# One PSUM bank taken from the product with V, given to scores and transpositions, and a plan with slack on banks

## The chip, the core and the metric

The kernel runs on one core of a Trainium2 chip. Its time is the device time of one execution in microseconds (us). TensorE (PE) does matmuls and transpositions and writes them to PSUM, which has eight banks of 512 fp32 columns; VectorE (DVE) and ScalarE (ACT) read PSUM; GpSimd (POOL) works in SBUF alone; SyncE (SP) issues the DMAs. Each engine runs its instructions in the order in which the program holds them, and waits there for what it needs.

## What is computed

Causal attention with a decay bias, over 4 batches, 8 heads, 576 positions and 64 dimensions a head, and then a mixture of 4 experts in which each token takes all of them, weighted by `domain_probs`:

```python
scores = q @ k.transpose(0, 1, 3, 2) / np.sqrt(D)
cum = np.cumsum(np.maximum(s, 0.0), axis=-1)
bias = -(cum[:, :, :, None] - cum[:, :, None, :])
scores = np.where(causal, -1e9, scores + np.minimum(bias, 0.0))
attn = exp(scores - max); attn = attn / (attn.sum(-1) + 1e-9)
x = (attn @ v) as 2304 rows of 8 * 64
p = domain_probs / (domain_probs.sum(-1) + 1e-9)
out = sum over e of p[:, e] * (relu(x @ w1[e]) @ w2[e])      # w1 512x1024, w2 1024x512
```

## The kernel before

**Visits.** Attention goes in 40 visits. The first 8 treat rows 0 to 319 of the heads of batch 0, the next 8 the other rows of these heads, and the last 24 a whole head each. A visit has up to five row blocks. For each block TensorE computes scores into a bank `S` (L584 or L587; blocks of 576 columns in two pieces of 288), VectorE adds the mask and takes the maximum (L597), ScalarE takes the exponential and its sum (L605), GpSimd or VectorE adds 1e-9 to the sum (L611), VectorE inverts it (L613), and GpSimd, ScalarE or VectorE multiplies the block by it (L400 to L402). TensorE then transposes the block's 128x128 pieces into a bank `T` (L632). ScalarE copies the rounded high part `aTh` from it (L407) and VectorE subtracts for the low part `aTl` (L660, L663); with that the bank is free.

**Product with V.** When all of a visit's blocks are transposed, TensorE multiplies by V (L686). `V` holds the high part of V in 64 columns and the low part in the other 64, so the result has two halves, that are added: ScalarE copies one from PSUM into `xr` (L696), VectorE adds the other (L701). A visit of 576 rows doesn't fit one bank of 512 columns, so the tile `pv` has two banks, with its first 256 columns at the end of the first; each V block's product is cut at column 256. Two heads make a pair; its `xr` is split in two parts (`xh`) and stored to `x_d`.

**Between them.** The first expert's two layers (L778 and L791, in banks `mo`), over groups of two or three tiles of tokens, fill TensorE where attention waits. Their inputs `xg` are loaded from `x_d` (L771).

**What sets the order.** The order of all these instructions is not written by hand. A planner (`Sched.run`) plays the tasks through with a duration for each and, on every engine, takes the ready task of the lowest `prio`; what it takes is written at once into the program. A task takes banks from pools and gives them back; a bank given back is free again in the plan 150 ns after the task's end (L286). `sources` says from which pools a bank may come: `S` and `T` have two banks each, and may take a bank `mo` while no filler matmul is ready. The planner stops when attention is done. The rest of the first expert's work is written behind it, with the preparation of the other experts' operands on GpSimd (`sums_of`: for the Strassen-like scheme of those experts GpSimd forms four sums for each of three groups of six tiles, twelve in all, each split in two parts; SP stores each at L916, and loads `xf_d` into `t` at L899 and `x_d` into `x` at L872 for them) placed at fixed counts of matmul time behind the end of attention. Then the other three experts follow, on TensorE without breaks.

Of the kernel before, what the change touches and what calls it, by code (L numbers as in the profile page):

```python
# [57 lines left out]
def t_pe4(n):  # L58
    return max(n / 0.6, 157) + 3
# [6 lines left out]
def t_dve(n):  # L66
    return n / 0.96 + 70
# [20 lines left out]
D6 = 3000  # L88
NWARM = 7
# [65 lines left out]
class Sched:  # L155
# [32 lines left out]
    def sources(self, t, p, lend):  # L188
        if p in ("S", "T") and lend:
            return (p, "mo")  # L190
        if t.prio < 1000.0 * NH + 900:
            return LEND.get(p, (p,))
        return (p,)

    def run(self, until):
# [22 lines left out]
        while left:  # L218
# [3 lines left out]
            for e in names:  # L222
# [62 lines left out]
                for p, k in t.give:  # L285
                    self.pools[self.home.pop((p, k))].append([end + 150, self.tok.pop((p, k))])  # L286
# [18 lines left out]
def body(ctx, tc, qk, vp, s, dp, w1, w1s, w2, w2s, out):  # L305
# [39 lines left out]
    make("pv", 1, [P, 1024], pool=pattn)  # L345
# [152 lines left out]
    prev_v = prev_ad = None  # L498
    for j, (h, ms) in enumerate(VISITS):
# [9 lines left out]
        pv0 = 256 if ext > 512 else 0  # L509
# [158 lines left out]
        mms = []  # L668
        for aT in (aTh, aTl)[0:1 if first else 2]:
            for n in range(nb):  # L670
                if aT is aTl and n == NC - 1:
                    continue
                i0 = max(q0, 128 * n)
# [4 lines left out]
        def f(e, j=j, mms=mms, first=first, pvk=pvk, o=o, pv0=pv0):  # L678
            t = tok[pvk]
            for i, (aT, n, i0, i1) in enumerate(mms):  # L680
                same = [k for k, x in enumerate(mms) if pv0 == 0 or (x[2] >= 256) == (i0 >= 256)]
                if first:
                    st, mv = tok[f"vz{j % 2}", j][:, n, :], tok["aTf", j][:, n, i0:i1]
                else:
                    st, mv = tok["V", j][:, n, :], aT_blocks(aT, tok["par", j], n, n + 1, i0, i1)[:, 0, :]
                nc.tensor.matmul(t[:, pv0 + i0:pv0 + i1], st, mv, start=(i == same[0] and not (first and o)),  # L686
                                 stop=(i == same[-1] and (not first or o > 0)))
        cost = sum(t_pe4(w - u) if first else t_pe(w - u) for _, _, u, w in mms)
        v = sch.add({"PE": cost}, f, evs + [v_ready] + ([prev_v] if first and o else []), prio=base + PO,
                    take=[pvk] if not (first and o) else [], give=[(f"vz{j % 2}", j), ("aTf", j)] if first else [("V", j), ("par", j)])  # L690
        prev_v = v

        r0, r1 = q0, ext
        if not first:
            def f(e, j=j, o=o, r0=r0, r1=r1, pk=pk, pv0=pv0):
                nc.scalar.activation(tok["xr", pk][o:o + 64, r0:r1], tok["pv", j][64 - o:128 - o, pv0 + r0:pv0 + r1], AF.Copy)  # L696
            sh = sch.add({"ACT": t_act(r1 - r0)}, f, [v], prio=base + PO + 10, take=[("xr", pk)] if o == 0 else [])

            def f(e, j=j, o=o, r0=r0, r1=r1, pk=pk, pv0=pv0):
                xr = tok["xr", pk]  # L700
                nc.vector.tensor_tensor(out=xr[o:o + 64, r0:r1], in0=tok["pv", j][o:o + 64, pv0 + r0:pv0 + r1], in1=xr[o:o + 64, r0:r1], op=ALU.add)  # L701
            ad = sch.add({"DVE": t_dve(r1 - r0)}, f, [sh], prio=base + PO + 10, give=[("pv", j)])
        else:
            ad = v
        attn.append(ad)
        if o:
# [3 lines left out]
            def xsrc(pk=pk, r0=r0, r1=r1, first=first, pv0=pv0):  # L710
                return tok["pv", pk][:, pv0 + r0:pv0 + r1] if first else tok["xr", pk][:, r0:r1]
# [570 lines left out]
```

## Time and profile before

| | |
|---|---|
| median of 3 runs | 937.98 us (937.55 to 938.73) |
| the profiled execution | 939.92 us, span 938.1 |
| PE busy in the span | 926.4 us (99%), 6304 matmuls |
| DVE, ACT, POOL busy | 713.6 (76%), 451.6 (48%), 456.8 us (49%) |
| mean granted clock | 0.998 |

A row of the profile names an engine, the line of the kernel, the operation and its tiles (buffer numbers left out), with starts in us from the span's start. `PE` is a matmul, `PEld` the load of its weights, which runs ahead. A matmul's row is longer than the step to the next matmul, since matmuls overlap; their pace is read from the starts. Idle time in brackets is that of the engine just before the instruction, with what ended it. Fp32 matmuls have two rows each in the counts.

### The profile page before, as it was taken

Reading aid. Unit: us, or ns where it says so; the run is one execution under the profiler, and the core shown is the slowest. Engines: PE = TensorE matmul, PEld = TensorE weight load, DVE = VectorE, ACT = ScalarE, POOL = GpSimd, SP = SyncE. Lnnn points to the kernel's source line nnn. Section 1 sums busy time; section 2 is a strip of 40 time slices with the busy share of each in tenths; the row PEclk is TensorE's granted clock in tenths of the full one; section 3 lists DMA queues with packets and bytes.
Section 4 is the critical chain, followed back from the end, with each engine's and each line's share of the span. In section 5 each row is a group of like instructions: output and inputs, shape, how many; then the busy total and the mean of one; then the engine's idle time right before and its main releaser. Section 6 shows DMA issues by size and latency. Waiting matters only on the chain.

```text
span 938.1 us, 17970 instructions
## 1 busy us (share of the span) xinstructions
PE 926.4 (99%) x6304; PEld 882.1 (94%) x6304; DVE 713.6 (76%) x1727; ACT 451.6 (48%) x1036; POOL 456.8 (49%) x503
## 2 busy tenths in 40 slices
PE   9989999999999999999999999999999999999998
PEld 6878898998999988999999999999999999999998
DVE  7978888888886211468779977988797879678976
ACT  6878887787775110252444333434252524443340
POOL 5557575475541689412753173435343714571222
PEclk9999999999999999999999999999999999999999
DMA  5877678677642796596775558654785458744603
GB/s 141 251 209 213 191 184 239 172 207 207 164 125 85 240 388 217 190 318 243 236 240 184 189 185 281 214 177 160 247 279 186 142 197 275 235 154 152 221 30 118
DMA packets 125898, 189.71 MB, mean 202 GB/s; under 512 B 10433, under 2 KB 102113, under 8 KB 125809
## 3 DMA queue, kind: packets, MB, share of 16 engines
q1 hardware_dynamic: 125808, 188.57, 63.3%
q8 instruction: 50, 0.82, 0.4%
q14 instruction: 40, 0.32, 0.1%
HBM read 144.73 MB, written 29.54 MB: 186 GB/s over the span
## 4 chain that ended last, share of the span: by engine, by line
PE 87%; DVE 4%; DMA 3%; issue 2%; ACT 2%; POOL 1%; SPq 0%; DVEq 0%; POOLq 0%; ACTq 0%
PE pb L1079 26%; PE pb L1089 20%; PE mo L1089 8%; PE mo L791 7%; PE mo L778 6%; PE T L632 5%; PE pv L686 5%; PE S L587 4%; PE pb L778 3%; PE pb L791 2%; DMA xg<-x_d 1%; PE S L584 1%; DVE a L597 1%; DVE aTl L660 1%; DMA raw<-in_qk_dram 1%
## 5 line engine op out<-in xcount | busy, mean ns | idle before, releaser
L1079 PE MATMUL pb<-x,w1h 128*128 128x384 f32 x1008 | 256.6, 335 | 0.5 <-ACT t L1119 0.3
L1079 PEld LDWEIGHTS pb<-x,w1h 128*128 128x128 f32 x1008 | 180.8, 188 | 2.5 <-DVE t L1123 1.8
L1079 PE MATMUL pb<-x,w1l 128*128 128x384 f32 x504 | 168.5, 334 | 0.0
L394 POOL TENSOR_TENSOR hT_r<-t,hT_r 128x768 fp32r<-128x768 f32 x18 | 34.0, 1887 | 268.5 <-PE pb L1079 215.5
L1119 ACT ACTIVATE t<-pb 128x384 f32<-128x384 f32 x144 | 66.3, 486 | 160.8 <-PE pb L1079 151.6
L1182 DVE SCALAR_TENSOR_TENSOR acc<-pb,prob,acc 128x256 f32<-128x256 f32 x288 | 126.2, 476 | 5.3 <-PE pb L1089 4.9
L1089 PE MATMUL pb<-w2h,hT_r 128*128 128x256 f32 x720 | 114.6, 283 | 0.1
L402 POOL TENSOR_SCALAR a<-a,sm 128x192 f32<-128x192 f32 (+4 forms) x145 | 83.9, 586 | 57.2 <-DVE sm L613 39.5
L605 ACT ACTIVATE a<-a,mx 64x64 f32<-64x64 f32 (+4 forms) x160 | 89.1, 559 | 23.0 <-DVE mx L597 16.6
L1089 PEld LDWEIGHTS pb<-w2h,hT_r 128*128 128x128 f32 x720 | 99.5, 191 | 0.3 <-issue 0.3
L1123 DVE TENSOR_TENSOR t<-pb,t 128x384 f32<-128x384 f32 x108 | 54.4, 550 | 57.5 <-PE pb L1079 36.1
L1079 PEld LDWEIGHTS pb<-x,w1l 128*128 128x128 f32 x504 | 94.6, 188 | 0.0
L1096 ACT ACTIVATE hT_r<-t 128x768 fp32r<-128x768 f32 x54 | 45.7, 846 | 98.1 <-PE pb L1089 92.6
L1093 DVE SCALAR_TENSOR_TENSOR t<-t 128x768 f32<-128x768 f32 x72 | 88.2, 1226 | 1.7 <-issue 1.6
L778 PE MATMUL mo<-xg,w1h 128*128 128x256 f32 (+1 forms) x368 | 84.9, 309 | 0.0
L407 ACT ACTIVATE aTh<-T 128x256 fp32r<-128x256 f32 (+2 forms) x167 | 65.8, 433 | 22.3 <-PE T L632 17.6
L632 PE MATMUL T<-idn,a 128*128 128x128 f32 x465 | 72.8, 278 | 3.7 <-DVE aTl L660 2.0
L660 DVE TENSOR_TENSOR aTl<-T,aTh 128x256 fp32r<-128x256 f32 (+2 forms) x167 | 72.5, 456 | 5.3 <-ACT aTh L407 4.0
L1089 PE MATMUL pb<-w2l,hT_r 128*128 128x256 f32 x360 | 71.5, 283 | 0.0
L597 DVE CUSTOM_DVE_ANT_0 a<-S,mask 128x320 f32<-128x320 f32 (+4 forms) x151 | 61.6, 420 | 9.7 <-PE S L584 4.4
L632 PEld LDWEIGHTS T<-idn,a 128*128 128x128 f32 x465 | 53.2, 142 | 15.5 <-issue 4.6
L1182 DVE SCALAR_TENSOR_TENSOR acc<-mo,prob,acc 128x256 f32<-128x256 f32 x144 | 62.9, 476 | 1.6 <-PE mo L1089 1.6
(149 smaller groups left out, 2076.3 us busy)
## 6 DMA issues: line engine op xcount, KB each, us to landing
x<-xs_d SPq DMA_DIRECT2D x68, 768.0 KB
x<-x_d SPq DMA_DIRECT2D x55, 768.0 KB
xs_d<-x SPq DMA_DIRECT2D x12, 768.0 KB
raw<-in_qk_dram SPq DMA_DIRECT2D x24, 288.0 KB
KK<-AB_r SPq DMA_DIRECT2D x24, 288.0 KB
x_d<-xh SPq DMA_DIRECT2D x12, 576.0 KB
w1r<-in_w1s_dram SPq DMA_DIRECT2D x6, 1024.0 KB
w2r<-in_w2s_dram SPq DMA_DIRECT2D x6, 1024.0 KB
```

The costliest lines, as they stand in the source:

```text
L402: (nc.gpsimd if e == "POOL" else nc.vector).tensor_scalar(out, in_, scale, 1.0 if bias is None else bias, op0=ALU.mult, op1=ALU.mult if bi ...
L597: nc.vector.tensor_tensor_reduce(out=z[0:n, j0:j1], in0=tok["S", (c, pi)][0:n, 0:j1 - j0], in1=mask[0:n, 448 - a + j0:448 - a + j1], scale ...
L605: nc.scalar.activation(z[0:n, 0:bb], z[0:n, 0:bb], AF.Exp, bias=tok["mx", c][0:n, k:k + 1], scale=-1.0, accum_out=tok["sm", c][0:n])
L632: nc.tensor.transpose(t[:, 128 * k:128 * k + 128], z[:, 128 * x:128 * x + 128], idn)
L660: nc.vector.tensor_tensor(out=dst, in0=src, in1=h_.bitcast(F32), op=ALU.subtract)
L778: nc.tensor.matmul(t[:, 0:w], wl[q][:, dc, o:o + P], xgt[:, l, dc, 0:w], start=(u == 0), stop=(u == 3 * KD - 1))
L791: nc.tensor.matmul(t, ht[:, fc, 128 * ti:128 * ti + 128], wl[fc // 2][:, fc % 2, :], start=(u == 0), stop=(u == 3 * KF - 1))
L1079: nc.tensor.matmul(ts[u][:, 0:TG], wv[wl][:, k, 128 * u:128 * u + 128], x[:, xl_, k, :], start=start and k == 0 and n == 0, stop=k == 1 an ...
L1089: nc.tensor.matmul(ts[t][:, 0:256], h_part(o, hl_)[:, k, 128 * t:128 * t + 128], wv[wl][:, k, :], start=start and k == 0 and n == 0, stop= ...
L1093: (nc.gpsimd if e == "POOL" else nc.vector).scalar_tensor_tensor(out=out, in0=in0, scalar=0.0, in1=in1, op0=ALU.max, op1=op)
L1119: nc.scalar.activation(tmp[name][:, u], ts[u][:, 0:TG], f)
L1182: nc.vector.scalar_tensor_tensor(out=a_, in0=ts[t][:, 0:256], scalar=prob[:, tt, e:e + 1], in1=a_, op0=ALU.mult, op1=ALU.add)
```

## The change

The tile `pv` shrinks to one bank, and the bank set free makes a pool `X` of its own, from which `S` and `T` may take. The product of a visit of 576 rows is done in two tasks: columns 64 to 575 (512 of them, in `pv`) and then columns 0 to 63, which only the first V block reaches, in a bank of `T` (or `X`, or `mo`). Each has its own copy and add. `prev_ad` becomes a list, so that the pair's split waits for both adds. In the plan a bank of `S`, `T`, `X` or `mo` is free 500 ns and not 150 after the task that gives it back, from 45 us of the plan's time on.

```diff
+SPARE = ("S", "T")
+BSLACK = 500
+T_SLACK = 45000
+PSUM_POOLS = ("S", "T", "X", "mo")
...
     def sources(self, t, p, lend):
-        if p in ("S", "T") and lend:
-            return (p, "mo")
+        if p in ("S", "T") and (lend or p in SPARE):
+            return (p,) + ("X",) * (p in SPARE) + ("mo",) * lend
...
-                    self.pools[self.home.pop((p, k))].append([end + 150, self.tok.pop((p, k))])
+                    self.pools[self.home.pop((p, k))].append([end + (BSLACK if p in PSUM_POOLS and now > T_SLACK else 150), self.tok.pop((p, k))])
...
-    make("pv", 1, [P, 1024], pool=pattn)
+    make("pv", 1, [P, 512], pool=pattn)
+    make("X", 1, [P, 512], pool=pattn)
...
-        pv0 = 256 if ext > 512 else 0
+        cut = 64 if ext > 512 else 0
...
-                for u, w in ((i0, min(256, ext)), (max(256, i0), ext)) if pv0 else ((i0, ext),):
-                    if u < w:
-                        mms.append((aT, n, u, w))
...
+        spans = [(max(cut, q0), ext)] + [(0, cut)] * (cut > q0)
+        ads = []
+        v = None
+        for si, (r0, r1) in enumerate(spans):
+            mms = [(aT, n, max(r0, 128 * n), r1) for aT in (aTh, aTl)[0:1 if first else 2] for n in range(nb)
+                   if max(r0, 128 * n) < r1 and not (aT is aTl and n == NC - 1)]
+            bk = ("T", (j, "s")) if si else pvk
...
+                    nc.tensor.matmul(t[:, i0 - c0:i1 - c0], st, mv, start=(i == 0 and not (first and o)),
+                                     stop=(i == len(mms) - 1 and (not first or o > 0)))
...
+            v = sch.add({"PE": cost}, f, evs + [v_ready, v] + ([prev_v] if first and o else []), prio=base + PO,
+                        take=[bk] if not (first and o) else [], give=([(f"vz{j % 2}", j), ("aTf", j)] if first else [("V", j), ("par", j)]) if lastv else [])
...
+                nc.scalar.activation(tok["xr", pk][o:o + 64, r0:r1], tok[bk][64 - o:128 - o, r0 - c0:r1 - c0], AF.Copy)
+            sh = sch.add({"ACT": t_act(r1 - r0)}, f, [v] + ads, prio=base + PO + 10, take=[("xr", pk)] if o == 0 and si == 0 else [])
...
+                nc.vector.tensor_tensor(out=xr[o:o + 64, r0:r1], in0=tok[bk][o:o + 64, r0 - c0:r1 - c0], in1=xr[o:o + 64, r0:r1], op=ALU.add)
+            ads.append(sch.add({"DVE": t_dve(r1 - r0)}, f, [sh], prio=base + PO + 10, give=[bk]))
```

The new planning moves instructions on every engine from the start on. Three places show it; line numbers of the changed kernel are four or so higher.

On TensorE, the end of one product with V in the middle of attention, before (`V_116` is the V tile, `pv_101` the product's PSUM tile, `aTh` and `aTl` the parts of the transposed block; x2 is two in a row):

```order
L686 MATMUL pv_101<-aTh,V_116 128x64
L686 MATMUL pv_101<-aTl,V_116 128x256
L686 MATMUL pv_101<-aTl,V_116 128x320
L686 MATMUL pv_101<-aTl,V_116 128x128
L686 MATMUL pv_101<-aTl,V_116 128x320 x2
L686 MATMUL pv_101<-aTl,V_116 128x192
L632 MATMUL T_100<-idn,a_0_121 128x128 x2
L632 MATMUL T_99<-idn,a_0_123 128x128 x3
L587 MATMUL S_97<-KK_111,AB_r 128x448 x2
```

and the same visit's product now (its `a_0` tiles have numbers one higher, `X_102` is the new bank):

```order
L688 MATMUL pv_101<-aTh,V_117 128x64
L688 MATMUL pv_101<-aTl,V_117 128x512
L688 MATMUL pv_101<-aTl,V_117 128x448
L688 MATMUL pv_101<-aTl,V_117 128x320
L688 MATMUL pv_101<-aTl,V_117 128x192
L688 MATMUL X_102<-aTh,V_117 128x64
L688 MATMUL X_102<-aTl,V_117 128x64
L637 MATMUL T_99<-idn,a_0_122 128x128 x2
L592 MATMUL S_98<-KK_112,AB_r 128x192 x2
L592 MATMUL S_97<-KK_112,AB_r 128x320 x2
L637 MATMUL T_100<-idn,a_0_124 128x128 x3
L782 MATMUL mo_103<-xg,w1h_80 128x384
```

The cut at 256 is gone: the five and more pieces of `aTl` are four, of 512 to 192 columns, and two matmuls of 64 columns write into another bank behind them. The transpositions and scores behind the product go to other banks and stand in another order.

On ScalarE, around the second cast of a loaded `raw` tile, before (`AB_r` is the cast; the first cast is the first row):

```order
L407 ACTIVATE AB_r<-raw_104 128x576
L407 ACTIVATE aTh<-T_100 128x2x128
L605 ACTIVATE a_1_126,sm_147<-a_1_126,mx_141 128x448
L407 ACTIVATE aTh<-T_99 128x3x128
L781 ACTIVATE hT_r<-mo_103 128x256
L400 ACTIVATE a_0_127<-a_0_127,sm_145 128x576
L605 ACTIVATE a_1_128,sm_148<-a_1_128,mx_140 128x576
L696 ACTIVATE xr_131<-pv_101 64x256
L407 ACTIVATE AB_r<-raw_105 128x576
L407 ACTIVATE aTh<-T_100 128x4x128
```

and now, where the first cast stands 8 rows above the first of these:

```order
L412 ACTIVATE aTh<-X_102 128x4x128
L610 ACTIVATE a_0_126,sm_150<-a_0_126,mx_143 128x448
L699 ACTIVATE xr_132<-pv_101 64x256
L412 ACTIVATE aTh<-T_100 128x2x128
L412 ACTIVATE aTh<-T_99 128x3x128
L785 ACTIVATE hT_r<-mo_103 128x256
L412 ACTIVATE xh_133<-xr_132 128x256
L412 ACTIVATE aTh<-X_102 128x4x128
L412 ACTIVATE AB_r<-raw_106 128x576
L412 ACTIVATE aTh<-T_100 128x2x128
L412 ACTIVATE AB_r<-raw_105 128x576
L412 ACTIVATE V_116<-vraw_114 128x5x64
```

The second cast has moved from 8 to 16 rows behind the first, and the third, which was on GpSimd, stands two rows behind it.

On SP, the DMAs issued behind attention, before (`xs_d<-x` stores one of GpSimd's sums, `t` and `x` are its inputs, `xg` a block of the first expert's input):

```order
L899 DMA t<-xf_d_156 128x2x384 x2
L771 DMA xg<-x_d 128x2x256 x4
L899 DMA t<-xf_d_156 128x2x384 x2
L916 DMA xs_d<-x 128x4x384 x2
L899 DMA t<-xf_d_157 128x2x384 x2
L945 DMA w1r<-in_w1s_dram 128x4x512
L950 DMA w2r<-in_w2s_dram 128x4x512
L916 DMA xs_d<-x 128x4x384
L899 DMA t<-xf_d_157 128x2x384 x2
L771 DMA xg<-x_d 128x2x384 x4
L916 DMA xs_d<-x 128x4x384 x3
L872 DMA x<-x_d 128x4x384 x4
```

and now:

```order
L903 DMA t<-xf_d_157 128x2x384 x4
L920 DMA xs_d<-x 128x4x384 x2
L903 DMA t<-xf_d_158 128x2x384 x2
L775 DMA xg<-x_d 128x2x256 x4
L949 DMA w1r<-in_w1s_dram 128x4x512
L954 DMA w2r<-in_w2s_dram 128x4x512
L920 DMA xs_d<-x 128x4x384
L903 DMA t<-xf_d_158 128x2x384 x2
L920 DMA xs_d<-x 128x4x384 x3
L876 DMA x<-x_d 128x4x384 x4
L920 DMA xs_d<-x 128x4x384
L775 DMA xg<-x_d 128x2x384 x4
```

The `xg` loads have moved back against the stores: the one of 384 columns stood behind three of them and stands behind seven and the four `x` loads. In the whole, TensorE had 426 first-layer and 216 second-layer matmuls ahead of the last product with V, and has 384 and 169.

## Rows read from the trace of the kernel before

**Rows 1.** Stretches: length, busy us of engines (x instructions), granted clock, DMA share, GB/s

```profile
70.00:300.00 230.00, 228.94 (x1577) 209.24 (x1576) 192.06 (x714) 179.14 (x504) 130.59 (x262) 1.00 0.64 180
...
65.20:68.80 3.60, 3.60 (x13) 2.81 (x14) 2.73 (x11) 3.11 (x8) 1.05 (x3) 0.53 0.50 137
```

**Rows 2.** Waits of the weight loads, 70 to 300 us: total us, times, longest

```profile
PEld T L632 <- issue: 4.6, 14, 0.6
PEld S L587 <- DVE mx L597: 1.2, 5, 0.4
PEld T L632 <- DVE aTl L660: 1.0, 4, 0.5
```

**Rows 3.** Timeline at 211 us: start, us, engine, line, operation, tiles

```profile
211.10 0.61 PE L791 MATMUL mo<-w2l,hT_r 128*128 128x512 f32 x2
...
211.37 0.89 DVE L660 TENSOR_TENSOR aTl<-T,aTh 128x256 fp32r<-128x256 f32 x2
...
211.94 0.87 PE L632 MATMUL T<-idn,a 128*128 128x128 f32 x6 [0.22 <-DVE aTl L660]
```

**Rows 4.** Waits of TensorE, 0 to 70 us

```profile
PE T L632 <- DVE aTl L660: 1.6, 1, 1.6
```

**Rows 5.** Timeline of ScalarE at 63 us

```profile
63.23 0.68 ACT L407 ACTIVATE AB_r<-raw 128x576 fp32r<-128x576 f32 x1 [1.72 <-DMA raw<-in_qk_dram]
```

**Rows 6.** Groups by form, 70 to 300 us: busy us, mean ns, idle before

```profile
L701 DVE TENSOR_TENSOR xr<-pv,xr 64x576 f32<-64x576 f32 x23 | 17.3, 754 | 3.9 <-ACT xr L696 3.2
...
L663 DVE TENSOR_TENSOR aTh<-T,aTh 64x64 fp32r<-64x64 f32 x27 | 5.9, 218 | 0.4
```

**Rows 7.** Timeline of TensorE, one product with V and what follows

```profile
107.81 0.97 PE L686 MATMUL pv<-aTh,V 128*128 128x256 f32 x7
...
109.46 0.71 PE L632 MATMUL T<-idn,a 128*128 128x128 f32 x5
109.93 0.54 PE L587 MATMUL S<-KK,AB_r 128*128 128x320 f32 x2
```

**Rows 8.** Timeline of TensorE, end of attention and filler behind it

```profile
300.17 0.42 PE L778 MATMUL mo<-xg,w1h 128*128 128x256 f32 x2
...
303.85 0.40 PE L778 MATMUL pb<-xg,w1h 128*128 128x256 f32 x2
...
306.73 3.82 PE L791 MATMUL pb<-w2h,hT_r 128*128 128x512 f32 x16
310.38 1.98 PE L791 MATMUL pb<-w2l,hT_r 128*128 128x512 f32 x8
```

**Rows 9.** Timeline of TensorE, first layer of the three-tile block

```profile
340.06 0.57 PE L778 MATMUL pb<-xg,w1h 128*128 128x384 f32 x2
...
343.16 0.62 PE L778 MATMUL pb<-xg,w1h 128*128 128x384 f32 x2 [0.27 <-DMA xg<-x_d]
...
343.79 0.51 PE L778 MATMUL mo<-xg,w1h 128*128 128x384 f32 x2
...
344.31 0.51 PE L778 MATMUL mo<-xg,w1h 128*128 128x384 f32 x2
```

**Rows 10.** Timeline of GpSimd, behind its fifth and its seventh sum

```profile
337.94 1.84 POOL L883 TENSOR_TENSOR t<-t 128x768 f32<-128x768 f32 x1 [2.63 <-DMA t<-xf_d]
...
347.19 1.29 POOL L883 TENSOR_TENSOR t<-w1r 128x512 f32<-128x512 f32 x1
```

**Rows 11.** Timeline of SP's queue

```profile
329.03 5.69 SPq L771 DMA_DIRECT2D xg<-x_d  x4
...
343.04 4.66 SPq L872 DMA_DIRECT2D x<-x_d  x4
347.80 1.86 SPq L916 DMA_DIRECT2D xs_d<-x  x1
```

**Rows 12.** A stretch behind attention

```profile
326.00:356.00 30.00, 29.23 (x159) 26.24 (x158) 6.12 (x11) 4.11 (x9) 26.36 (x20) 1.00 1.06 386
```

**Rows 13.** Normalisation of the widest block, by form

```profile
L402 POOL TENSOR_SCALAR a<-a,sm 128x576 f32<-128x576 f32 x29 | 23.7, 818 | 6.5 <-DVE sm L613 5.2 <-DVE sm L611 0.2
```

More of the change, by code (lines that the diff above doesn't have):

```diff
@@ L667, in body @@
         pvk = ("pv", pk if first else j)
[L668 to L673, printed above, removed]
-                for u, w in ((i0, min(256, ext)), (max(256, i0), ext)) if pv0 else ((i0, ext),):
-                    if u < w:
-                        mms.append((aT, n, u, w))
[L678 to L687, printed above, removed]
@@ L688, in body, with f @@
-        cost = sum(t_pe4(w - u) if first else t_pe(w - u) for _, _, u, w in mms)
-        v = sch.add({"PE": cost}, f, evs + [v_ready] + ([prev_v] if first and o else []), prio=base + PO,
-                    take=[pvk] if not (first and o) else [], give=[(f"vz{j % 2}", j), ("aTf", j)] if first else [("V", j), ("par", j)])
+        spans = [(max(cut, q0), ext)] + [(0, cut)] * (cut > q0)
[5 more added lines that the diff above has]
+            bk = ("T", (j, "s")) if si else pvk
+            def f(e, j=j, mms=mms, first=first, bk=bk, o=o, c0=r0 if si else cut):
+                t = tok[bk]
+                for i, (aT, n, i0, i1) in enumerate(mms):
+                    if first:
+                        st, mv = tok[f"vz{j % 2}", j][:, n, :], tok["aTf", j][:, n, i0:i1]
+                    else:
+                        st, mv = tok["V", j][:, n, :], aT_blocks(aT, tok["par", j], n, n + 1, i0, i1)[:, 0, :]
+                    nc.tensor.matmul(t[:, i0 - c0:i1 - c0], st, mv, start=(i == 0 and not (first and o)),
+                                     stop=(i == len(mms) - 1 and (not first or o > 0)))
+            cost = sum(t_pe4(w - u) if first else t_pe(w - u) for _, _, u, w in mms)
+            lastv = si == len(spans) - 1
+            v = sch.add({"PE": cost}, f, evs + [v_ready, v] + ([prev_v] if first and o else []), prio=base + PO,
+                        take=[bk] if not (first and o) else [], give=([(f"vz{j % 2}", j), ("aTf", j)] if first else [("V", j), ("par", j)]) if lastv else [])
+            if first:
+                ads.append(v)
+                continue
+            def f(e, j=j, o=o, r0=r0, r1=r1, pk=pk, bk=bk, c0=r0 if si else cut):
+                nc.scalar.activation(tok["xr", pk][o:o + 64, r0:r1], tok[bk][64 - o:128 - o, r0 - c0:r1 - c0], AF.Copy)
+            sh = sch.add({"ACT": t_act(r1 - r0)}, f, [v] + ads, prio=base + PO + 10, take=[("xr", pk)] if o == 0 and si == 0 else [])
+            def f(e, j=j, o=o, r0=r0, r1=r1, pk=pk, bk=bk, c0=r0 if si else cut):
+                xr = tok["xr", pk]
+                nc.vector.tensor_tensor(out=xr[o:o + 64, r0:r1], in0=tok[bk][o:o + 64, r0 - c0:r1 - c0], in1=xr[o:o + 64, r0:r1], op=ALU.add)
+            ads.append(sch.add({"DVE": t_dve(r1 - r0)}, f, [sh], prio=base + PO + 10, give=[bk]))
@@ L691, in body @@
         prev_v = v
         r0, r1 = q0, ext
[L694 to L704, printed above, removed]
+        ad = ads[-1]
@@ L729, in f @@
                             nc.sync.dma_start(out=t[64 * hh - 64:64 * hh + 64, u - g * NP:w - g * NP], in_=xsrc()[:, u - b * S - r0:w - b * S - r0])
-                attn.append(sch.add({"SP": 500}, f, [ad, prev_ad], prio=base - XD, give=[("xr", pk)], xfer=(r1 - r0) * 512, follow=xl))
+                attn.append(sch.add({"SP": 500}, f, ads + prev_ad, prio=base - XD, give=[("xr", pk)], xfer=(r1 - r0) * 512, follow=xl))
             def f(e, b=b, hh=hh, r0=r0, r1=r1, pk=pk, first=first):
@@ L741, in body @@
                 g0_xl.append(xl)
[L742 removed]
+        prev_ad = ads
     def load_w(e, which, i, t):
```

9 lines of the change are left out of this document (4 added, 5 removed).

## The prediction

> **What bounds the kernel now.** I read the stretches first: from 70 to 300 us, where the attention visits run with matmuls of the first expert between them, TensorE is busy 228.94 of 230 us [rows 1]. After that it is as full. The total is therefore TensorE's work plus what it loses, and the change neither adds nor removes a matmul of weight. What it can win is lost time, so I looked for that next. The busy figure hides most of it, because a matmul's end is modelled; the weight loads show it better. In that stretch they stood still before transpositions and scores for 4.6, 1.2 and 1.0 us, 23 waits and 6.8 us in all [rows 2]. One of them in order of time [rows 3]: the last second-layer matmul pair starts at 211.10, so its second at 211.33, and at the pace of such matmuls (16 in 306.73 to 310.38, 228 ns each, [rows 8]) the next could start at 211.56. The transposition starts at 211.94, 0.38 us late, right behind VectorE's two `aTl` subtractions that read the bank it writes. That is a bank wait. It is one of the larger ones.
>
> Before 70 us there is one large case: TensorE waits 1.6 us for `aTl` [rows 4], because ScalarE, which runs in order, stood 1.72 us before the cast of a `raw` load that landed at 63.2 us, with the `aTh` copy of the bank behind it [rows 5]. Right behind it stands a stretch of 3.60 us with a granted clock of 0.53, so about 1.2 GHz in place of 2.4 [rows 1], which is some 1.7 us of work lost (3.6 x 0.47).
>
> **The change, part by part.**
>
> *A, bank waits.* A third bank for scores and transpositions, and a plan that hands a bank on 350 ns later than it did (500 for 150, once past 45 us of its own time). Waits of 0.1 to 0.4 us are what such slack covers. How much of the 6.8 us of idle weight loads is lost by TensorE? The longest of these waits, 0.6 us [rows 2], is the one just read, of which 0.38 us was lost, some 62%; 62% of 6.8 is 4.2 us. I take 4.0 as won, with bounds 0 (the plan uses the bank to run the visits tighter, so the waits come back) and 6.8 (all of it, [rows 2]).
>
> *B, the early wait.* Its price is 1.6 us and the 1.7 us at half clock, 3.3 in all [rows 1, 4]. In the order of ScalarE the second `raw` cast stands 8 rows behind the first before and 16 now, so the load has longer to land; but a third cast now stands two rows behind that, with an `aTh` copy two rows further, and it can wait in the same way. I take a third of the gain, -1.0, bounds -3.3 (both gone) and +2.0 (the new third cast waits as long as the old second).
>
> *C, after attention.* Ahead of the last product with V the plan now places 553 filler matmuls where it placed 642: 42 first-layer matmuls (120 ns: 24 from 303.85 to 306.73, [rows 8]) and 47 second-layer ones (228 ns) less, 5.0 + 10.7 = 15.7 us. They are not saved, they run behind attention, whose last product was over at 300.2, where the next matmul starts [rows 8], and should now end some 16 us, plus the other gains earlier. So what waits there moves. Before, the load of the three-tile block (`xg`, 4 x 0.39 MB) was issued at 329.03 [rows 11] and landed late: its first layer shows a quarter per 1.03 us, 340.06 to 343.16 for three [rows 9], where an undisturbed quarter takes 0.52 (343.79 to 344.31), so 1.6 us were lost. Now that load stands in SP's queue behind seven stores of GpSimd's sums and the four `x` loads, and not behind three. Counted from the end of attention, TensorE wants it after 47 + 48 + 48 second-layer and 2 x 96 first-layer matmuls, 143 x 0.228 + 192 x 0.120 = 55.6 us. GpSimd finished its seventh sum 47.0 us behind attention (347.19 less 300.2, [rows 10]), the four `x` loads were issued from 343.04, 42.8 us behind it, and took 4.66 us, and the store after them went at 347.80 [rows 11]. `x` loads, that store and the block are 3.15 + 0.79 + 1.57 = 5.5 MB; at the 386 GB/s that the queue moved from 326 to 356 us [rows 12] that is 14.3 us, so the last quarter lands at 57.1. TensorE wants that quarter at 55.6 + 3 x 0.52 = 57.2. It is a tie on these numbers; but the second pair of `t` loads, for which GpSimd waited 2.63 us [rows 10], now has one more block load of 1.05 MB ahead of it (2.7 us). So I take a wait of 2.8 us against the 1.6 that goes: +1.2. Bounds -1.6 (no wait) and +4.4 (6 us).
>
> *D, the product itself.* 13 matmuls become 11 with the same 3136 columns. 13 take 1.65 us (107.81 to 109.46, [rows 7]), of which the columns at 2.4 GHz are 1.31. Two large ones fewer gain at most 0.05 us, two separate ones of 64 columns cost at most what a transposition of 128 takes, 0.1 us each (five in 0.47, [rows 7]). 24 visits: 0, bounds -1.2 and +2.
>
> *E, evacuation and chain.* Each full visit's copy and add of 576 columns become one of 512 and one of 64. A 576-wide add takes 754 ns, 1.3 a column, a 64 x 64 operation 218 [rows 6]; the pair costs 218 - 64 x 1.3 = 0.13 us more, on ScalarE about the same, 3.2 us over 24 visits on each. VectorE is busy 192 of 230 us, ScalarE 179 [rows 1], so it lies beside TensorE; if that cover were gone it would cost up to 3.2 us. The Trainium skill, page Perfetto Trace Analysis, section Optimizing Scalar/DVE Operations, speaks against such a split: it gives VectorE about 125 ns for each further operation on PSUM and ScalarE 51 ns. By that page the sum would be 3.0 and 1.2 us of engine time, no more than the rows give.
> What is late next when banks wait no longer is the softmax: a transposition needs its normalised block, whose last step alone takes 818 ns on GpSimd [rows 13]. Counted in the two orders with the paces above, the TensorE work between a block's last score and its first transposition falls from 10.1 to 6.9 us (median of the later visits). I take +0.8 for such waits, bounds 0 and +7.
>
> **Sum**, against the profiled execution (939.92 us, span 938.1 and 1.8 around it): -4.0 - 1.0 + 1.2 + 0 + 0.8 = -3.0, so 936.9. That execution stood 1.94 above the median of the runs, 937.98; the same step from the median is 935.0. 0.2%, about what a measurement of this kernel can tell from no change, is 1.9 us.
>
> **The rivals.**
> 1. *The waits only change their reason*: transpositions wait for their normalised block instead of for their bank. E is +4.0 and cancels A: -4.0 - 1.0 + 1.2 + 4.0 = +0.2. For it: that distance falls by a third, and slack is kept on banks alone. Against it: neither VectorE nor ScalarE is full. 938.2 us. Beside it the page Perfetto Trace Analysis of the Trainium skill, section Matmul Optimizations, asks that all eight PSUM banks be used; both kernels hold eight (2 + 2 + 2 + 2, now 2 + 2 + 1 + 1 + 2), so by that rule alone nothing is won.
> 2. *Slower: the block load behind seven stores.* Place: SP's queue, 44 to 60 us behind attention. If GpSimd's seventh sum comes 6 us later than 47.0, the load is 6 us later too: a wait of 8.8 us, and as behind the 1.6 us wait [rows 1, 4] a stretch at half clock, 1.7. That is 8.8 + 1.7 - 1.6 = 8.9 for C, and a sum of -4.0 - 1.0 + 8.9 + 0.8 = +4.7: 942.7 us. It decides the sign from C = 4.2 on. For it: the DMA queue is full there [rows 12]. Against it: GpSimd does the same seven sums at the same distance from the end of attention. The Trainium skill, page DMA: Bandwidth & Descriptors, section Queues, rings and completion order, says that descriptors are consumed in ring order on each DMA engine; by that rule the load can't pass the stores ahead of it. Rows 9 agree, with quarters landing one after the other.
> 3. *The plan does not do what it says*: the third bank is taken by the 64-column products, so banks are as short as before. A is 0, the sum +1.0: 939.0 us.
>
> **How the numbers follow.** Forecast (A to E as taken) 0.54, own range 931 to 936.5; rival 1 0.24; rival 2 0.12; rival 3 0.10. The forecast's spread reaches below 936.1 in nearly all of it and rival 1 now and then: faster 0.57. Within 0.2% (936.1 to 939.9): most of rivals 1 and 3, 0.27. Slower: rival 2 and the edge of rivals 1 and 3, 0.16. For 8 in 10 the range runs from 930.5 (A near its bound, B gone) to 939.8.
>
> **What would show it.** A: in the visits, idle weight loads before transpositions and scores behind VectorE fall from 6.8 to 2 or 3 us. B: no stretch with a granted clock near 0.5 between 60 and 75 us. C: attention ends between 278 and 286 us; a wait of the first layer for `xg` some 56 us behind that end. D: a product's 11 matmuls take 1.6 to 1.75 us. E: waits of transpositions for GpSimd's normalisation under 1 us in total. I am wrong if waits for normalised blocks add up to more than 4 us, or if the `xg` wait is over 6.

## The result: 946.69 us, slower, and where the time went

The changed kernel takes 946.69 us (944.51 to 949.14, four runs) against 937.97 for the kernel before: ratio 1.0093, 95% interval 1.0077 to 1.0110. I had forecast 935.0. Its profiled execution is the fastest of the four, 944.51 us with a span of 942.4 us, 4.3 us over the span of before. Executions of one kernel differ in TensorE's clock: "full clock" below means a mean granted clock of 0.999 or 1.0 (the expectations say undisturbed), and four executions of 995.64, 1113.83, 3191.26 and 3191.32 us, far above the others of their kernels, are left out of the medians.

"Filler" is a matmul of the first expert's two layers that the plan puts between the visits of attention; what isn't placed there runs behind it.

| us of the span | before | changed | difference |
|---|---|---|---|
| start to the end of attention | 300.17 | 283.21 | -16.96 |
| of it filler that moved behind attention (42 x 0.119 + 47 x 0.227) | | | -15.67 |
| so attention itself | | | **-1.3** |
| end of attention to the first matmul of expert 1 | 96.96 | 118.34 | +21.38, net of filler **+5.7** |
| from there to the end | 541.0 | 540.8 | -0.1 |

The sum is right to 0.1 us, so the question has two halves: why attention gained 1.3 us and not the 4.2 of the forecast, and what the 5.7 us behind it are. Matmul starts give a third view, used below: **a filler matmul of the first layer takes 119 ns (256 columns) or 173 (384), one of the second layer 227 (512); the start of a matmul less all the filler ahead of it is the time that attention itself has taken so far.**

**Behind attention.** Timeline of TensorE's matmuls and weight loads (start, us, engine, line, operation, tiles; in brackets the idle time before), to be held against [rows 9]:

```profile
337.00 1.98 PE L795 MATMUL pb<-w2l,hT_r 128*128 128x512 f32 x8
343.65 1.01 PE L782 MATMUL pb<-xg,w1h 128*128 128x384 f32 x2 [4.68 <-DMA xg<-x_d]
344.78 0.94 PE L782 MATMUL pb<-xg,w1h 128*128 128x384 f32 x2
...
344.72 0.50 PEld L782 LDWEIGHTS pb<-xg,w1h 128*128 128x128 f32 x2 [0.24 <-DMA xg<-x_d]
...
346.77 0.50 PEld L782 LDWEIGHTS pb<-xg,w1h 128*128 128x128 f32 x2 [0.20 <-DMA xg<-x_d]
```

SP's queue and GpSimd, to be held against [rows 10, 11], and two stretches (length, busy us of PE, PEld, DVE, ACT, POOL, granted clock, DMA share, GB/s):

```profile
327.17 3.56 SPq L876 DMA_DIRECT2D x<-x_d  x4
331.40 1.44 SPq L920 DMA_DIRECT2D xs_d<-x  x1
332.89 4.78 SPq L775 DMA_DIRECT2D xg<-x_d  x4
...
331.33 1.29 POOL L887 TENSOR_TENSOR t<-w1r 128x512 f32<-128x512 f32 x1
...
327.00:346.80 19.80, 15.12 (x66) 12.24 (x66) 2.35 (x4) 0.50 (x2) 19.30 (x14) 0.87 1.01 350
341.40:348.20 6.80, 4.54 (x13) 3.90 (x14) 0.00 (x0) 0.07 (x1) 6.80 (x4) 0.52 0.92 335
```

The first quarter of the three-tile block makes TensorE wait 4.7 us. The others land 1.02 to 1.07 us apart, as they did before, the last at 346.77, 63.6 us behind attention. Beside that the clock is near 1.2 GHz, half of the full 2.4, from 341.4 to 348.2 us. Half speed alone costs less than the 2.3 us that 4.54 busy us suggest: up to 346.8 TensorE's pace, 1.1 us a quarter, is the pace at which quarters land, and only the last 1.4 us are slow for no other reason.

**In the visits.** Weight loads' waits (total us, times, longest), to be held against [rows 2], and the same stretch's busy times, against the first of [rows 1]:

```profile
PEld T L637 <- POOL a L407: 2.8, 10, 0.6
PEld T L637 <- issue: 1.6, 6, 0.4
PEld S L592 <- DVE mx L602: 1.5, 5, 0.4
PEld X L592 <- DVE aTl L665: 0.7, 2, 0.5
PEld X L637 <- POOL sm L616: 0.6, 2, 0.3
PEld X L637 <- POOL a L407: 0.6, 2, 0.4
PEld X L637 <- issue: 0.3, 2, 0.2
...
70.00:283.20 213.20, 211.73 (x1428) 192.38 (x1427) 188.83 (x716) 176.69 (x512) 128.40 (x269) 1.00 0.68 188
```

Waits for banks (`issue`, `mx`, `aTl`) are 4.1 us where they were 6.8, and GpSimd's normalised blocks and sums now end 4.0 us of waits. In the kernel before GpSimd ended 1.2 us of them, in two rows that stand beside the three of [rows 2]:

```profile
PEld T L632 <- POOL V L394: 0.9, 3, 0.4
PEld T L632 <- POOL sm L611: 0.3, 1, 0.3
```

So all waits of the weight loads come to 8.1 us, and came to 8.0. VectorE is busy 188.83 of 213.2 us, 89%, where it was 84%.

### The profile page after: what moved, and what is told of

It is laid out like the page before. It is cut to its first block, busy times and chain, and to the rows that moved or that the text cites. A ratio compares the mean times of both kernels' runs of the same rounds, so it can differ in the third digit from the quotient of the medians.

```text
span 942.4 us, 17842 instructions
## 1 busy us (share of the span) xinstructions
PE 927.9 (98%) x6256; PEld 880.9 (93%) x6256; DVE 713.9 (76%) x1742; ACT 454.2 (48%) x1056; POOL 460.7 (49%) x516
## 4 chain that ended last, share of the span: by engine, by line
PE 85%; DVE 5%; DMA 3%; ACT 2%; issue 2%; POOL 2%; SPq 0%; DVEq 0%; POOLq 0%; ACTq 0%
PE pb L1083 26%; PE pb L1093 20%; PE mo L1093 8%; PE mo L795 7%; PE mo L782 5%; PE pb L782 4%; PE pv L688 4%; PE T L637 3%; PE S L592 3%; PE pb L795 3%; DMA AB_f<-cx 1%; DVE aTl L665 1%; DMA xg<-x_d 1%; PE X L637 1%; DVE a L602 1%
## 5 line engine op out<-in xcount | busy, mean ns | idle before, releaser
L407 POOL TENSOR_SCALAR a<-a,sm 128x448 f32<-128x448 f32 (+4 forms) x149 | 83.3, 564 | 57.6 <-DVE sm L618 37.3
L782 PE MATMUL mo<-xg,w1h 128*128 128x256 f32 (+1 forms) x336 | 77.6, 309 | 0.0
L1097 DVE SCALAR_TENSOR_TENSOR hT_r<-t,hT_r 128x768 fp32r<-128x768 f32 x54 | 56.8, 1053 | 7.6 <-ACT hT_r L1100 7.1
L637 PE MATMUL T<-idn,a 128*128 128x128 f32 x328 | 56.9, 278 | 0.9 <-POOL a L407 0.6
L782 PEld LDWEIGHTS mo<-xg,w1h 128*128 128x128 f32 x336 | 56.4, 191 | 1.2 <-issue 0.6
L602 DVE CUSTOM_DVE_ANT_0 a<-S,mask 128x448 f32<-128x448 f32 (+4 forms) x128 | 51.9, 417 | 7.5 <-PE S L589 5.3
L665 DVE TENSOR_TENSOR aTl<-T,aTh 128x256 fp32r<-128x256 f32 (+3 forms) x119 | 53.3, 454 | 4.2 <-ACT aTh L412 3.2
```

The source lines that it names most:

```text
L407: (nc.gpsimd if e == "POOL" else nc.vector).tensor_scalar(out, in_, scale, 1.0 if bias is None else bias, op0=ALU.mult, op1=ALU.mult if bi ...
L602: nc.vector.tensor_tensor_reduce(out=z[0:n, j0:j1], in0=tok["S", (c, pi)][0:n, 0:j1 - j0], in1=mask[0:n, 448 - a + j0:448 - a + j1], scale ...
L637: nc.tensor.transpose(t[:, 128 * k:128 * k + 128], z[:, 128 * x:128 * x + 128], idn)
L665: nc.vector.tensor_tensor(out=dst, in0=src, in1=h_.bitcast(F32), op=ALU.subtract)
L782: nc.tensor.matmul(t[:, 0:w], wl[q][:, dc, o:o + P], xgt[:, l, dc, 0:w], start=(u == 0), stop=(u == 3 * KD - 1))
L1097: (nc.gpsimd if e == "POOL" else nc.vector).scalar_tensor_tensor(out=out, in0=in0, scalar=0.0, in1=in1, op0=ALU.max, op1=op)
```

## Experiments

Each kernel was timed between runs of the kernel before. **anchor** counts the preparation steps from a place in the first expert's matmuls. In all anchored kernels the line is

```diff
-    spent = 0.0
+    left = <matmul time of the first expert still to be written, us>
+    spent = 91.97 - left
```

where 91.97 is what was left in the kernel before (107.29 in the changed one, both by the plan's durations), and a step is written when `spent` reaches its due time.

| kernel | median (at full clock), us | ratio to before, 95% interval | attention net of filler, early / late visits | lost behind attention |
|---|---|---|---|---|
| before | 938.3 to 938.5, three sittings | 1 | +1.5 / +1.4 | 2.1 |
| changed | 946.69 | 1.0093 (1.0077 to 1.0110) | -1.6 / -0.5 | 7.8 |
| anchor | 938.32 (937.2) | 0.9998 (0.9979 to 1.0017) | +1.2 / +2.3 | 0.5 |
| after_late | 938.07 (937.4) | 1.0004 (0.9989 to 1.0019) | -2.5 / -1.2 | 0.6 |
| before_late3 | **936.66** (936.6) | 0.9977 (0.9965 to 0.9989) | 0 / 0 | 0.4 |
| anchor_s150 | 940.23 (940.0) | 1.0023 (1.0006 to 1.0040) | +3.4 / +6.6 | 1.3 |
| anchor_s800 | 942.51 (939.9) | 1.0036 (1.0021 to 1.0050) | +3.0 / +5.5 | 0.5 |
| anchor_lag | 940.28 (938.3) | 1.0013 (0.9997 to 1.0030) | +3.7 / +5.9 | 0.5 |
| split_only | 944.81 (944.8) | 1.0073 (1.0058 to 1.0088) | -0.7 / +7.1 | 0.6 |
| anchor_nospare | 955.01 | 1.0171 (1.0150 to 1.0193) | -2.6 / +9.7 | 8.9 |
| before_s500 | 947.16 | 1.0090 (1.0076 to 1.0104) | -4.0 / +1.9 | 9.2 |
| late_x45 | 937.54 (937.5) | 0.9984 (0.9975 to 0.9993) | -2.0 / 0.0 | 0.5 |
| late_noadd | 938.53 (936.4) | 0.9997 (0.9985 to 1.0010) | +3.4 / +2.4 | 0.7 |

The column on attention is against before_late3, whose attention has the same instructions in the same order as the kernel before; it is read at the ends of the products of full visits 2 to 5 and 21 to 24, averaged. "Lost behind attention" is the stretch up to expert 1 less its matmuls at the three paces. Both come from one profiled execution each, half-clock stretches included. The changed kernel, anchor and after_late hold the same attention, and their three profiles lose 1.1, 1.1 and 1.3 us from the early to the late visits: the loss between them repeats to 0.2 us, where the level differs by 3.7.

**What the 5.7 us are: the order in SP's queue.** First the anchored kernel.

> The changed kernel with one edit behind attention: the preparation steps are counted not from the end of attention but from the place in the first expert's remaining matmuls where the kernel before had them, so SP's queue stands in the old order again (the three-tile block behind three stores, not behind seven and four loads). Theory 1, the place of that load in SP's queue costs the time: the stretch from the end of attention to the first matmul of expert 1, 118.34 us in the changed kernel and 96.96 + 15.7 = 112.7 by the kernel before, is 112.5 to 113.5; no half clock behind the load; what is left is the gain of attention, 1.3 us, so 936.7 us (935.5 to 938), and the runs agree within 1.5 us where they were 4.6 us apart. Theory 2, the load is late because attention ends 17 us earlier and the same bytes have to pass (the queue is full wherever the load stands): the stretch stays over 116 us and the time over 942.

Measured: the stretch is 111.05 us, 0.5 lost, the median 938.32; at full clock 937.2. The load stands behind three stores again, and TensorE doesn't wait for it:

```profile
329.83 2.94 SPq L775 DMA_DIRECT2D xg<-x_d  x4
333.22 8.46 SPq L920 DMA_DIRECT2D xs_d<-x  x3
341.73 4.66 SPq L876 DMA_DIRECT2D x<-x_d  x4
...
341.62 0.51 PE L782 MATMUL pb<-xg,w1h 128*128 128x384 f32 x2
```

Theory 1 holds, theory 2 falls; the stretch came out 1.5 us under its range, since what the kernel before loses there (2.1) went too. But the runs spread wider than expected, 935.3 to 943.8: 5 of 12 executions had a mean clock of 0.996 or less. Next, one number in the changed kernel:

```diff
-T_PREP = (0.0, 18.0, 37.0)
+T_PREP = (0.0, 18.0, 44.0)
```

> The changed kernel with one number changed: the third group of preparation steps begins 44 and not 37 us of matmul time behind attention. In SP's queue the three-tile block then still stands behind all seven stores, and is issued no earlier than the seventh sum allows (331.4 us in the changed kernel, it was issued at 332.9), but the four loads of 3.15 MB stand behind it. Theory 1a, the bytes ahead of the load are the price: at 380 GB/s the block lands 3 to 5 us after its issue, by 337, before TensorE wants it at 338.8; the wait of 4.7 us and the half clock behind it are gone, 936 to 938.5 in undisturbed runs. Theory 1b, the stores are (as the second rival of the prediction has it: the seventh sum is late): the wait stays at 3 us or more and the time over 940.

Measured: 938.07, at full clock 937.4; 8.6 us under the changed kernel. Its SP queue and TensorE:

```profile
313.25 17.95 SPq L920 DMA_DIRECT2D xs_d<-x  x4
331.30 2.78 SPq L775 DMA_DIRECT2D xg<-x_d  x4
334.13 3.45 SPq L876 DMA_DIRECT2D x<-x_d  x4
...
338.11 0.51 PE L782 MATMUL pb<-xg,w1h 128*128 128x384 f32 x2
```

The load is issued at 331.30, only 1.6 us earlier than in the changed kernel and still behind all seven stores, and TensorE does not wait. Theory 1a holds: **the 3.15 MB of `x` loads ahead of the block were the price, not the stores and not GpSimd's sums.** GpSimd stood just as long before its sixth sum (4.87 us, 4.85 in the changed kernel).

Is that a gain of the change? The kernel before, with its preparation steps 3 us later:

```diff
-    spent = 0.0
+    spent = -3.0
```

> The kernel before with the preparation steps begun 3 us of matmul time later; in SP's queue this moves the three-tile block ahead of one pair of temporary loads, and nothing else. In the anchored kernel the stretch from attention's end to expert 1 lost 0.5 us where the kernel before loses 2.1. Theory 1, that is the place of the load against GpSimd's stores and loads and has nothing to do with the change: the waits of TensorE for the block (0.8 us in matmuls, 1.9 in weight loads) go and 0.8 to 1.6 us are won, 936.6 to 937.4. Rival: the anchored kernel has it from the earlier end of attention; here the time stays within 0.4 us of the kernel before.

Measured: 936.66, the lowest median of all; nothing waits for the block. Theory 1 holds: the 1.6 us that the anchored kernels save behind attention are to be had without the change. In this profile the wait of [rows 4] is there again, and no half clock follows it:

```profile
65.08 0.55 PE L632 MATMUL T<-idn,a 128*128 128x128 f32 x3 [1.31 <-DVE aTl L660]
...
60.00:70.00 10.00, 8.69 (x60) 7.26 (x60) 8.60 (x25) 7.90 (x20) 4.96 (x10) 1.00 0.72 202
```

So the stretch at half clock in the profile before [rows 1] was that execution's, not the kernel's: of the 85 runs of before in three sittings, eight had a mean clock of 0.998 or less.

**What attention gains.** Split, bank and slack one at a time; first the split and nothing else (`SPARE = ()`, `BSLACK = 150`, anchored).

> The split of the product alone: the anchored kernel with 150 ns of slack and the bank X used by nobody. 415 + 216 filler matmuls ahead of the last product. Theory D, the split is free (a product's matmuls took 1.64 us where they took 1.66): attention net of filler within 1 us of the kernel before, and with the tail of the anchored kernel 936.5 to 939. Rival: with one bank the next product waits for the copy and add of the one before it, and the 64 columns take a bank of T: 1 us and more of waits of the product for ScalarE and VectorE, and over 940.

Measured: 944.81; the visits lose 7.8 us between the early and the late ones. Its waits from 80 us to the end of attention:

```profile
PEld T L637 <- issue: 7.9, 20, 1.5
PEld S L592 <- DVE mx L602: 3.0, 11, 0.8
```

and of TensorE itself from 70 us on:

```profile
PE T L637 <- DVE xr L704: 1.6, 3, 1.2
```

The rival holds, though not by the next product: the 64 columns sit in a bank of `T` until VectorE has added them (`xr`), and transpositions wait. The split is not free; my term D counted its matmuls alone. With the bank `X`, still without slack:

> As the anchored kernel, but the plan gives a bank back 150 ns after its task, as before, at all times: only the split of the product and the third bank are left. Theory A, as in the prediction: slack is what covers waits for banks; without it weight loads of transpositions and scores stand still behind VectorE as before (some 6 us from 80 us to the end of attention), and the time is 2 to 4 us over the anchored one, 939 to 941. Theory A2, three banks for scores and transpositions are enough by themselves: bank waits as in the anchored kernel, time within 1 us of it. Theory A3, the slack itself costs (it holds banks back that are free, so scores start late): 1 to 2 us under the anchored one.

Measured: 940.23, 2.8 us over the anchored kernel at full clock. A holds in size, against A2 and A3, and weight loads stand 5.5 us for banks where the anchored kernel has 3.8: the bank pays back most of the split (4.8 us of 7.6 at full clock against the anchored kernel), slack the rest (2.8). More slack does not go on winning (`BSLACK = 800`):

> The anchored kernel with a slack of 800 in place of 500 ns; the plan places 384 + 203 filler matmuls ahead of the last product with V, not 384 + 169. Theory A: the waits behind VectorE that are left from 80 us on (T and X behind its subtractions, S behind its maxima) go as well, 0.5 to 1.5 us under the anchored kernel, 935.7 to 936.7 in undisturbed runs. Theory E: what is left are waits for blocks, which slack on banks does not cover; within 0.5 us of the anchored kernel.

Measured: 942.51, 939.9 at full clock, so neither: 2.7 us worse. From 70 to 430 us the waits for blocks are the largest, as Theory E had it, but it expected no loss:

```profile
PEld T L637 <- POOL a L407: 5.0, 13, 0.8
```

Slack without the bank, with the split and without it (in the second, `+ 150` becomes 500 for `S`, `T`, `mo` from 45 us on in the kernel before):

> As the anchored kernel, but neither scores nor transpositions may take the bank X: the split of the product and the slack of 500 ns are left, the bank set free lies unused. The plan then places 480 + 218 filler matmuls ahead of the last product with V, so attention takes longer on the clock (294 to 302 us) with the filler in it. Theory E, the waits for normalised blocks (5.0 us of idle weight loads in the changed kernel, 1.8 before) come from visits run tighter with the third bank: here they fall under 2.5 us, and net of filler attention gains 2 to 4 us against the kernel before, 934 to 936. Theory E2, they come from the split product's copies and adds on ScalarE and VectorE, which stay: 4 us and more of such waits, 937 to 939.

> The kernel before with the slack of 500 ns alone (two banks for scores, two for transpositions, product with V in two banks as it was), its preparation steps anchored as in the anchored kernel. The plan places 480 + 219 filler matmuls ahead of the last product where the kernel before has 426 + 216. Theory A, slack is what saves waits for banks: from 80 us to the end of attention it gains 2 to 3 us net of filler, as slack did with the third bank (940.0 with 150 ns, 937.2 with 500, undisturbed runs): 935.5 to 937. Theory A4, slack is only to be had with a bank to spare: with two banks each the plan starves scores and transpositions, as in the kernel with the third bank unused (955.0), and the time is over 943.

Measured: 955.01 and 947.16. Their totals do not read attention alone: attention ends 15 and 7 us later on the clock while the anchor holds the preparation in place, so the three-tile block is late there too (waits of 3.8 and 4.4 us) and 8.9 and 9.2 us are lost behind attention. In the visits they lose 12.3 and 5.9 us, with a stretch at half clock in each. Theory E falls and A4 holds in direction. A slack of 300 without the bank:

> The kernel before with a slack of 300 ns and its own two banks each, with the three-tile block ahead of a pair of loads as in the late3 kernel: 409 + 216 filler matmuls ahead of the last product. In the run with 500 ns the first full visits were 3.8 us ahead of the kernel before, and it was lost at 160 us where banks ran out. If a little slack is to be had without the third bank, this beats the late3 kernel (936.6): 934 to 936. If slack without a spare bank starves the visits, 938 to 941.

Measured, with the anchor at 88.97: 942.26 (ratio 1.0039, 1.0026 to 1.0051), with a mean clock of 0.998 or less in 11 of 12 executions; no gain. Its profile is of the execution of 1113.83 us, so where this kernel waits stays open.

**Why the waits came back.** Slack for blocks as well as banks (`NLAG = 400`, in the anchored kernel):

```diff
-                    n.ready = max(n.ready, end + (LAG[e][0] if e in n.engs else LAG[e][1]))
+                    n.ready = max(n.ready, end + (LAG[e][0] if e in n.engs else LAG[e][1] + (NLAG if e == "POOL" and now > T_SLACK else 0)))
```

> As the anchored kernel, but the plan also counts 400 ns more, from 45 us of its time on, until another engine may use what GpSimd has made (normalised blocks above all): the slack is kept on blocks as well as on banks. The plan places 384 + 199 filler matmuls ahead of the last product. Theory E: transpositions lose time to blocks that the plan took to be ready too early; their waits for GpSimd fall from 5.0 us to under 2, and 2 to 3 us are won against the anchored kernel: 934 to 935. Rival: the waits move on to the bank or to scores, the time within 0.8 us of the anchored one.

Measured: 940.28, 938.3 at full clock, 1.1 over the anchored kernel. The waits for normalised blocks of GpSimd fell to 0.6 us, and others took their place, such as these from 70 us on:

```profile
PEld T L638 <- issue: 1.4, 3, 0.7
PEld T L638 <- ACT a L406: 1.3, 2, 0.7
PEld pv L689 <- DVE aTh L669: 1.0, 2, 0.8
```

Theory E falls as a remedy; the rival (the waits move on) is nearer. If the visits are tight on several engines, work taken off one of them should help:

> As the changed kernel with the third preparation group at 44 us, in the same order, but the 24 adds of 64 columns on VectorE are left out (so columns 0 to 63 of those heads lack one half of their sum). Theory E2, the extra work of the split on VectorE is why transpositions wait for blocks in the visits: 24 x 0.2 us less on VectorE gives 1 to 2 us, undisturbed runs at 935.5 to 936.5 where they were 937.4, and waits for blocks fall from 4.0 us to under 3. Theory E, they wait since the plan runs the visits tighter: no change, 937 to 938.

Measured: 936.4 at full clock (4 executions, 934.5 to 936.9) against 937.4 (8, 936.3 to 939.2); 938.53 over all, since 8 of its 12 executions had a mean clock of 0.996 or less (the profiled one of them had its stretch from 32 us). In the visits it gains 1.0 us from early to late where the three profiles with the adds lose 1.1 to 1.3. Waits of weight loads from 80 us to the end of attention, after_late, with 7.8 us in all:

```profile
PEld T L637 <- POOL a L407: 2.8, 10, 0.6
PEld T L637 <- issue: 1.6, 6, 0.4
PEld S L592 <- DVE mx L602: 1.4, 4, 0.5
```

and without the 24 adds, 4.9 us in all:

```profile
PEld T L637 <- POOL a L407: 2.1, 6, 0.6
PEld T L637 <- issue: 1.2, 4, 0.4
PEld S L592 <- DVE mx L602: 0.5, 2, 0.3
```

Waits for blocks and sums of GpSimd fall from 4.0 to 2.8 us. E2 holds in the visits: 24 adds of 0.22 us, 5.3 us of VectorE, cost 2.1 to 2.4 us there. The medians at full clock have 1.0 us, on ranges that overlap. The adds were not all under cover. They are more than what the split adds, since the 512-column add is shorter than the one of 576 was:

```profile
L704 DVE TENSOR_TENSOR xr<-pv,xr 64x512 f32<-64x512 f32 x23 | 15.8, 688 | 7.0 <-ACT xr L699 6.8
...
L704 DVE TENSOR_TENSOR xr<-T,xr 64x64 f32<-64x64 f32 x17 | 3.8, 221 | 1.0 <-ACT xr L699 0.5
```

688 + 221 ns for 754 [rows 6] is 0.155 us a visit, 3.7 us in all. The copies on ScalarE were not taken out, and what the rest of the waits for blocks comes from was not tested.

**Why executions differ.** The anchored kernel and after_late are the same program up to the end of attention, yet their profiles are 3.5 us apart there. Both wait at 30 us: first anchor, then after_late, each with its stretch from 26 to 45 us:

```profile
30.61 1.48 PE L589 MATMUL S<-AB_f 66*128 66x448 f32 x4 [1.34 <-DMA AB_f<-cx]
...
26.00:45.00 19.00, 17.61 (x82) 13.50 (x81) 12.33 (x39) 11.83 (x34) 9.54 (x16) 0.82 0.82 207
```

```profile
30.02 1.48 PE L589 MATMUL S<-AB_f 66*128 66x448 f32 x4 [0.72 <-DMA AB_f<-cx]
...
26.00:45.00 19.00, 18.24 (x108) 14.32 (x107) 16.29 (x50) 14.34 (x40) 12.32 (x19) 1.00 0.91 245
```

TensorE waits for a visit's decay row, and in the execution with the longer wait the clock is at half from 32.3 to 39.1 us:

```profile
32.30:39.10 6.80, 6.80 (x18) 4.78 (x16) 4.54 (x12) 3.29 (x9) 4.81 (x7) 0.50 0.86 226
```

The changed kernel's profile waited nearly as long and stayed at the full clock:

```profile
30.77 1.48 PE L589 MATMUL S<-AB_f 66*128 66x448 f32 x4 [1.25 <-DMA AB_f<-cx]
```

Seven kernels (these three, anchor_s150, anchor_s800, anchor_lag, late_noadd) have the same order of instructions up to 50 us, and this wait is 0.72, 1.00, 1.25, 1.34, 2.13, 2.46 and 2.58 us in their profiles: the load lands at another time in each. In the last four half clock begins between 31.6 and 33.8 us, in the one with 1.00 at 40.9 us, behind a second wait of 0.83; in the other two there is none.

To see whether the bank makes that wait, `X` is handed out from 45 us of the plan on (after_late with `sch.pools["X"][0][0] = 45000.0`):

> The changed kernel with its third preparation group at 44 us (as in the run before it) and with the bank X handed out only from 45 us of the plan's time on, so that the first visits are planned as in the kernel before. The plan places 384 + 196 filler matmuls ahead of the last product. In the profiles of the changed plan the second of the first visits waits 0.7 to 2.6 us for its decay row (the load of AB_f from cx) at 30 us, and in 18 of 52 undisturbed-tail executions a stretch at half clock follows; the kernel before has no such wait and 4 of 56 executions below a mean clock of 0.998. Theory F, the earlier use of X makes that wait: here the wait is gone, at most 1 or 2 of the executions show a lower clock, and the median comes to 936 to 937.5. Rival: the early gain of some 2.5 us goes with it, undisturbed runs at 938.5 to 940.

Measured: the wait is gone, all 12 executions have a mean clock of 0.999 or 1.0, the median is 937.54 (ratio 0.9984, 0.9975 to 0.9993):

```profile
26.00:45.00 19.00, 17.99 (x110) 14.47 (x109) 16.53 (x55) 15.28 (x43) 11.90 (x16) 1.00 0.82 240
```

Of the 72 executions of the six kernels of experiment with that order, 31 had a mean clock of 0.997 or less (the expectation counts 18 of 52); where the unprofiled ones lost it is not known. Theory F holds. At full clock it is no faster than after_late; what it wins is that no execution falls out.

## Why the prediction was wrong, step by step

*C, behind attention, is the step that failed most: +5.7 for +1.2, and over its bound of +4.4. A is the second: of the 7.3 us between forecast and measurement, profile against profile, C is 4.5 and attention, which is A, B, D and E together, 2.9.* The place and the moment were right: the matmul that wants the first quarter would have come at 338.8, 55.6 us behind attention, as worked out. The last quarter was to land at 57.1 and landed at 63.6. Three terms make the 6.5 us. The `x` loads were issued 44.0 and not 42.8 us behind the end: 1.2. From there to the landing 350 GB/s x 19.6 us = 6.9 MB went through and not 5.5. The other 1.4 MB must have been queued ahead of or beside these loads; the store of the sum before, which could not be issued before GpSimd was done at 326.7, is 0.8 of them, and the rest isn't told apart. At 386 GB/s they are 3.6 us. And the rate was 350 and not 386: 1.8. I had read when the loads were issued and had not asked what was still queued ahead of them; [rows 12], a DMA share of 1.06, says that the queue was full. A clock that falls behind such a wait I had put into rival 2 alone, though [rows 1, 4] show one behind 1.6 us; here it cost some 0.7. The prediction's sign of being wrong, an `xg` wait over 6 us, was set too high: a wait of 4.7 was enough.

*Rival 2 had the sign, not the mechanism.* It wanted GpSimd's seventh sum 6 us late; it was 48.1 us behind attention for 47.0. Its chance of 0.12 hung on the wrong engine: after_late leaves seven stores and the sum where they are. The sentence that called it "a tie on these numbers" was the warning: to land early could win no more than the 1.6 us, and to land late costs all of the delay. Its reading of [rows 9] proves less than it says: they show the quarters of one load, and nothing of a load and the stores ahead of it.

*A, bank waits: 0 net for -4.0.* Bank waits did fall, from 6.8 us to 4.1 and not to 2 or 3, and the sum of waits stayed the same: 7.7 us in before_late3, 7.8 in after_late, from 80 us to the end of attention. That is rival 1's mechanism. The row that spoke against it, VectorE busy 84% of the stretch, was read as cover. With 89 fillers fewer among the visits the same work of VectorE stands in 17 us less, 89% of the stretch. The run without the adds shows that a part of the new waits hangs on VectorE; that its share of busy time makes the rest is not shown.

*E, evacuation: taken as hidden, and it isn't.* The price on the engine was near (3.7 us for 3.2 on VectorE). That it "lies beside TensorE" was wrong: 5.3 us of such adds cost the visits 2.1 to 2.4, so the 3.7 us that the split adds cost up to that much. The other half of E, waits for normalised blocks, was +0.8 with under 1 us of waits; they came to 3.4 us, 4.0 with the sums, and did not pass the 4 us that the prediction set as its sign of being wrong. The Trainium skill (Perfetto Trace Analysis, Optimizing Scalar/DVE Operations) counts about 125 ns of overhead for each further operation on PSUM on VectorE, and the trace agrees with its direction (221 ns for 64 columns, where 1.3 ns a column would make 84); the share of a fixed cost in a 64-column add is not told apart here.

*B, early wait.* No half clock in 60 to 75 us, as said, but I had credited the change with what was an accident of the profiled execution: before_late3 has the same wait and no half clock. The changed plan does gain up to the first visits (2.5 us in after_late against before_late3; 1.6 in the changed kernel's profile, which waited 1.25 us for its decay row), and gives 1.1 to 1.3 us back in the visits. The step did not see the new early wait, for a decay row at 30 us: I looked at the casts on ScalarE and not at the order of loads.

*D, the product.* 11 matmuls from 102.96 to 104.59, 1.63 us: as forecast.

*The median.* Profile against profile the kernel lost 4.6 us, median against median 8.7. 1.9 of the rest is the kernel before's profiled execution, which stood that much above its median; 2.2 is the changed kernel's other runs, with mean clocks down to 0.993.

## What to carry over

When attention, or any producer, is made to end earlier, everything that was placed by counts behind its end moves against everything that was placed by program position; list each load that crosses another, and cost it by all bytes ahead of it at the rate of that stretch and by the first use. Before a bank or a slack is credited with the waits that it covers, look at what the next wait would be, and at the busy share of the engines that feed it: here, with VectorE at 84% of the stretch before, the waits changed their reason and their sum stayed. And take a profile of before again before a stretch at half clock in it is booked as the kernel's: here the repair of one due time alone (936.66 us) beat both kernels.

## What the runs showed of the chip

Waits of TensorE of much the same length had a stretch of half clock behind them in one execution and none in another of the same program up to there: 1.34 us with one, 1.25 and 0.72 without, at 30 us; 1.6 us with one in before and 1.31 without in before_late3, at 65 us. During the wait of 4.7 us the clock was halved for 6.8 us, as long as at 30 us; the stretch at 65 us in before was half as long. The five executions of the anchored kernel with a lower mean clock were 3.7 us longer than the seven at full clock (medians 940.9 and 937.2). A load of 1.57 MB behind 3.15 MB of loads had its last quarter 19.6 us after these were issued, with the queue at 350 GB/s.
